# One core, attention and two MLP layers in one kernel: layer 1's first weights get a buffer of their own and load 17 steps earlier; their conversion, some scores and some value products change step

## The chip, the cores and the metric

The kernel runs on one NeuronCore of a Trainium2 chip. The metric is the time of one execution on the device in microseconds, lower is better. The engines are named as in the profile: PE is TensorE (matmul, with PEld for its weight loads), DVE is VectorE, ACT is ScalarE, POOL is GpSimd, SP is SyncE, which here only issues DMAs. Each engine takes its instructions in the order in which they stand in its own queue, and waits at an instruction until the semaphores that it needs are there.

## The reference, cut to what matters

```python
def _attn_ref(q, k, v, w_pre, w_post):                 # batch 2, heads 12, sequence 448, head_dim 64
    scores = scale * np.matmul(q, k.transpose(0, 1, 3, 2))
    scores = np.einsum('bhij,hg->bgij', scores, w_pre)  # mix the heads before the softmax
    scores = scores - np.max(scores, axis=-1, keepdims=True)
    attn = np.exp(scores)
    attn = attn / (np.sum(attn, axis=-1, keepdims=True) + 1e-09)
    attn = np.einsum('bhij,hg->bgij', attn, w_post)     # and after it
    return np.matmul(attn, v)

def _moe_ref(x, w_in, w_out):                           # layer 1: 896 tokens, 768 -> 2048 -> 768
    h = x @ w_in
    g = h * np.clip(h + 3.0, 0.0, 6.0) / 6.0
    return g @ w_out

def _moe2_ref(x, w_in, w_out, a, b):                    # layer 2, the same sizes, a rational activation
    h = x @ w_in
    ...
    return (P / (Q + 1e-6)) @ w_out
```

`reference` runs the three after one another. The weights of the layers come as float64 words; the kernel reads them as pairs of int32.

## The kernel before

**Attention** is done in 46 steps `m`. A step handles 20 query rows (two groups of ten) of all 12 heads. Steps belong to eight chunks of up to 120 rows; chunks 0 to 7 begin at steps 0, 6, 12, 18, 23, 29, 35 and 41. In step m PE does, in this order: `premix(m)` (eight matmuls into the two banks `M`), then a part of a later chunk's scores (`sc`, two head pairs, eight matmuls) or of an earlier chunk's value products (`X`, 32 matmuls), then `postmix(m-2)` (64 matmuls into the bank `A`). There are two banks `M`, so the premix of step m+1 writes what the exp of step m has read.

Around a premix the chain is: DVE takes the row maxima of both banks (`st`, two reduces), ACT takes two exps (`e`), DVE inverts the sums (`norm`: two short instructions on `st`), POOL scales the second mix (`wr`), PE does the postmix two steps later, ACT copies its result out (`at`, the evacuation). X leaves its bank through ACT (`xh`) and DVE (`xl`). Scores leave theirs through DVE copies into one of two buffers `stage0`, `stage1` (chunk number modulo 2), and DMAs issued on SP spread the rows of a stage into `first`, a ring of five step inputs; the spread for step m+4 is issued in step m. A stage is written for chunk C+2 when the spreads of chunk C have read it.

**Layer 1** is done by units. Unit u of the first kind (u0, u1, ... the 16 column blocks of `w_in`) is 768 KB of raw words (`wraw`), which ACT and DVE turn into float32 and then into a high and a low part:

```python
nc.scalar.activation(out=w, in_=hw.bitcast(F32), func=AF.Copy, scale=2.0**-112)      # ACT wf
nc.vector.tensor_scalar(out=wi, in0=wi, scalar1=3, ..., op0=ALU.logical_shift_left)  # DVE, first of three on wf
```

Two more DVE instructions on `wf` follow (called the second and third), and then `wh` and `wl`: on POOL for the first four units, on ACT and DVE for the others. `split_pieces` is a generator, and `PIECES` says how many of its pieces each step runs at its end; `LOADS` says in which step the thirds of a raw unit are loaded. `gemm1(f, p)` multiplies unit f with the tokens of part p (384 or 512 of them): six times three matmuls, called `h1_f_p`. Unit u0's raw words take one of two buffers `wraw` in a pool `late`, which is made in step 37, when a pool with queries and keys is given back.

The order of the steps and of the tail behind them (the last two postmixes, the value products X7 of the last chunk, first matmuls of layer 1) is written out by hand. From `manual.__exit__` on a scheduler places the instructions; it may also put later ones between earlier ones of an engine's queue.

Of the kernel before, what the change touches and what calls it, by code (L numbers as in the profile page):

```python
# [29 lines left out]
NP = H // 2  # L30
# [18 lines left out]
def fused_kernel(  # L49
# [287 lines left out]

    THIRDS = 3

    def load_third(u, i):  # L340
        u = units[u]
        if i == 0:
            raws[u] = (pools["late"].tile([128, KD * 256], I32, tag="wraw", bufs=2, name="wraw"), KD)
        n = KD // THIRDS
        o = raws[u][0].rearrange("p (a b) -> p a b", b=256)[:, i * n : i * n + n]
        nc.sync.dma_start(out=o, in_=w1i[:, i * n : i * n + n, u[1] * 256 : u[1] * 256 + 256])

    def load_unit(u, eng=nc.sync):
        kind, i, kk = u
        if kind == "in2" and i in pre:  # L350
            t = ring("wpre")[:, : KD * 128].bitcast(F32)
            eng.dma_start(out=t, in_=pre[i])
            raws[u] = (t, KD)
            return
        if "gp2" in pools:
            t = ring("wraw")
        else:
            t = pools["late"].tile([128, KD * 256], I32, tag="wraw", bufs=2, name="wraw")
        cols = slice(i * 256, i * 256 + 256)
        if kind in ("in1", "in2"):  # L360
# [135 lines left out]
    def per_step(items):  # L496
# [24 lines left out]
    for m in range(len(pairs)):  # L521
# [33 lines left out]
        for p in xs[1::2]:  # L555
            p()
        if m == FREE:
            front.release()
            pools["late"] = tc.alloc_tile_pool(name="late", bufs=1, side="right", reuse_waits="tile")
            wpieces = (p for u in units[:4] for p in split_pieces(u))  # L560
# [26 lines left out]
    pieces(1)  # L587
    att.release()
# [290 lines left out]
```

## Time and profile before

| | |
|---|---|
| median of 3 runs | 666.91 us (666.86 to 667.76) |
| the profiled execution | 665.91 us, span from first to last instruction 664.2 us |
| PE busy | 645.7 us, 97% of the span |
| DVE, ACT, POOL busy | 77%, 57%, 5% |
| steps 0 to 45 | from 15.27 to 185.24 us |
| tail | from 185.24 to 201.64 us |
| from then on | h1_0_1 and all that follows |

The profile's rows give a start in microseconds of the span, a length, an engine, a source line and the tiles (the number behind a tile's name left out); what stands in square brackets is the idle time of that engine just before, and what ended it.

### The profile page before, as it was taken

The numbers are of one execution on the slowest core, as the hardware profiler recorded it, in microseconds if no ns is written. First come the engines' busy times: TensorE is split into PE (matmuls) and PEld (weight loads), VectorE is DVE, ScalarE is ACT, GpSimd is POOL, SyncE is SP. The second block draws the span as 40 slices with busy tenths as digits, with TensorE's granted clock in tenths as the row PEclk, the third lists the DMA queues.
The fourth block names the chain that finished last, engine by engine and source line by source line (L and its number), as shares of the span: only waits on it lengthen the run. The fifth ranks groups of instructions, "written<-read, shape, count | busy, mean of one in ns | idle before, by whom it ended". The sixth has DMA issues, their size and how long they took to land.

```text
span 664.2 us, 16127 instructions
## 1 busy us (share of the span) xinstructions
PE 645.7 (97%) x6681; PEld 537.2 (81%) x6682; DVE 514.2 (77%) x880; ACT 377.6 (57%) x682; POOL 34.2 (5%) x73
## 2 busy tenths in 40 slices
PE   8899999997899999999999999999999999999997
PEld 3355665664587988998888888899999999999997
DVE  5777677774658988889686665389998999989991
ACT  3666676765645555555333232167675676689851
POOL 2110110111312000000000000000000000000000
PEclk9999999997999999999999999999999999999999
DMA  6765544536344655556645233446757564746512
GB/s 220 239 198 190 149 179 138 169 131 194 124 134 141 204 167 167 173 183 211 198 140 173 88 119 98 164 170 235 250 174 278 192 229 161 273 156 214 190 49 95
DMA packets 72281, 115.48 MB, mean 174 GB/s; under 512 B 6352, under 2 KB 56816, under 8 KB 72208
## 3 DMA queue, kind: packets, MB, share of 16 engines
q1 hardware_dynamic: 71790, 114.08, 52.1%
q8 instruction: 52, 0.85, 0.5%
q10 hardware_dynamic: 418, 0.37, 0.2%
q14 instruction: 21, 0.17, 0.1%
HBM read 75.39 MB, written 19.27 MB: 143 GB/s over the span
## 4 chain that ended last, share of the span: by engine, by line
PE 89%; DVE 4%; ACT 3%; DMA 2%; issue 1%; POOL 0%; SPq 0%; POOLq 0%; DVEq 0%; ACTq 0%
PE h L318 11%; PE h L319 11%; PE h L320 11%; PE y L318 6%; PE y L320 6%; PE acc L318 6%; PE acc L320 6%; PE acc L319 6%; PE y L319 6%; PE sc L216 6%; PE A L275 5%; PE X L298 5%; PE M L232 5%; ACT e L241 1%; DMA first<-stage 1%
## 5 line engine op out<-in xcount | busy, mean ns | idle before, releaser
L318 PE MATMUL h<-xh,wh 128*128 128x512 f32 (+1 forms) x384 | 140.2, 365 | 0.9 <-DVE g L488 0.9
L319 PE MATMUL h<-xl,wh 128*128 128x512 f32 (+1 forms) x384 | 140.1, 365 | 0.0
L320 PE MATMUL h<-xh,wl 128*128 128x512 f32 (+1 forms) x384 | 139.1, 362 | 0.0
L318 PEld LDWEIGHTS h<-xh,wh 128*128 128x128 f32 x384 | 72.1, 188 | 9.4 <-issue 1.3
L320 PEld LDWEIGHTS h<-xh,wl 128*128 128x128 f32 x384 | 72.1, 188 | 8.1
L319 PEld LDWEIGHTS h<-xl,wh 128*128 128x128 f32 x384 | 72.2, 188 | 6.6
L239 DVE TENSOR_REDUCE st<-M 128x1 f32<-128x448 f32 x92 | 53.3, 619 | 30.9 <-PE M L232 30.5
L241 ACT ACTIVATE e<-M,st 128x448 f32<-128x448 f32 x92 | 57.5, 629 | 34.3 <-DVE st L239 34.3
L376 ACT ACTIVATE wf<-wraw 128x768 f32<-128x768 f32 (+1 forms) x56 | 49.5, 883 | 45.3 <-DVE wl L404 36.9
L403 ACT ACTIVATE wh<-wf 128x768 fp32r<-128x768 f32 (+1 forms) x52 | 42.5, 817 | 50.5 <-PE y L319 38.1
L320 PE MATMUL y<-gh,wl 128*128 128x384 f32 x192 | 70.6, 368 | 0.0
L318 PE MATMUL y<-gh,wh 128*128 128x384 f32 x192 | 70.5, 367 | 0.0
L319 PE MATMUL y<-gl,wh 128*128 128x384 f32 x192 | 69.9, 364 | 0.0
L404 DVE TENSOR_TENSOR wl<-wf,wh 128x768 fp32r<-128x768 f32 (+1 forms) x52 | 48.0, 923 | 27.4 <-ACT wh L403 27.3
L275 PEld LDWEIGHTS A<-wr,e 60*56 60x56 f32 x2944 | 43.6, 127 | 21.7 <-issue 18.7
L232 PE MATMUL M<-first,wp 60*64 60x448 f32 (+1 forms) x368 | 50.0, 554 | 8.1 <-ACT e L241 7.8
L283 ACT COPY at<-A 120x960 f32<-120x960 f32 x46 | 45.0, 978 | 22.4 <-PE A L275 21.6
L380 DVE SCALAR_TENSOR_TENSOR wf<-wraw,icst,wf 128x768 int32<-128x768 int32 (+1 forms) x56 | 55.3, 989 | 0.8
L384 DVE SCALAR_TENSOR_TENSOR wf<-wraw,icst,wf 128x768 int32<-128x768 int32 (+1 forms) x56 | 55.3, 988 | 0.7
L220 DVE COPY stage<-sc 120x448 f32<-120x448 f32 (+1 forms) x85 | 49.1, 616 | 7.2 <-PE sc L216 4.5
L275 PE MATMUL A<-wr,e 60*56 60x60 f32 x2944 | 49.7, 216 | 2.5 <-ACT at L283 2.2
L298 PEld LDWEIGHTS X<-at,vraw 120*64 120x64 f32 x768 | 38.3, 140 | 16.4 <-DVE st L249 7.0
(99 smaller groups left out, 1137.5 us busy)
## 6 DMA issues: line engine op xcount, KB each, us to landing
wraw<-in_moe_w_out_dram SPq DMA_DIRECT2D x28, 768.0 KB
first<-stage SPq DMA_DIRECT2D x92, 210.0 KB
wraw<-in_moe_w_in_dram SPq DMA_DIRECT2D x18, 768.0 KB
wpre<-in_moe_w_in_dram SPq DMA_DIRECT2D x10, 768.0 KB
w2h<-wh SPq DMA_DIRECT2D x16, 384.0 KB
w2l<-wl SPq DMA_DIRECT2D x16, 384.0 KB
ws<-w2h SPq DMA_DIRECT2D x16, 384.0 KB
ws<-w2l SPq DMA_DIRECT2D x16, 384.0 KB
```

The costliest lines, as they stand in the source:

```text
L220: return [lambda copy, i=i: copy(out=st[:n, i], in_=sc[i][:n, :S]) for i in range(2)]
L232: nc.tensor.matmul(mt[a][64 * c : 64 * c + 64, :S], lhsT=wp[o], rhs=src[o, c, :], start=True, stop=True,)
L239: nc.vector.tensor_reduce(out=st[:, a : a + 1], in_=mt[a][:, :S], op=ALU.max, axis=AX.X, negate=True)
L241: nc.scalar.activation(out=e[:, a], in_=mt[a][:, :S], func=AF.Exp, bias=st[:, a : a + 1], accum_out=st[:, 2 + a : 3 + a])
L275: nc.tensor.matmul(av[64 * c : 64 * c + JH, r, jc, :, a * HR : a * HR + HR], lhsT=e[o, a, j : j + JH], rhs=wr[o, a], start=True, stop=True,)
L298: nc.tensor.matmul(X[hh % 2 * D : hh % 2 * D + D, hh % 4 // 2, :n], lhsT=vs[:, jc, :], rhs=at[C][:, jc, hh, :n], start=(jc == 0), stop=(jc ...
L318: nc.tensor.matmul(o, lhsT=wh, rhs=mh, start=first, stop=False)
L319: nc.tensor.matmul(o, lhsT=wh, rhs=ml, start=False, stop=False)
L320: nc.tensor.matmul(o, lhsT=wl, rhs=mh, start=False, stop=last)
L376: nc.scalar.activation(out=w, in_=hw.bitcast(F32), func=AF.Copy, scale=2.0**-112)
L380: nc.vector.scalar_tensor_tensor(out=wi, in0=hw, scalar=icst[:, 0:1], in1=wi, op0=ALU.bitwise_and, op1=ALU.bitwise_or)
L384: nc.vector.scalar_tensor_tensor(out=wi, in0=lw, scalar=icst[:, 1:2], in1=wi, op0=ALU.logical_shift_right, op1=ALU.bitwise_or)
```

## The change

- `raw0`, a buffer that is there from the start. Raw units alternate between it and one buffer in `late`. u0's thirds are loaded in steps 20, 21 and 22, u1's in 37 and 38, u2's in 39 and 40, u3's in 42 and 43. A step's load is now issued on SP ahead of the step's spread.
- The pieces are cut otherwise: (ACT wf), (first DVE), (second DVE), (third DVE with wh and wl). `PIECES` runs two a step from step 37 to 42 and one each in 44 and 45. Only three units have wh and wl on POOL; u3's go to ACT and DVE.
- `FILL`: h1_0_0 is done in halves of nine matmuls, at the ends of steps 41 and 42. The tail is first half of h1_1_0, postmix 44, second half, postmix 45, h1_2_0, X7, h1_0_1. Before it was h1_0_0, postmix 44, half of h1_1_0, postmix 45, the other half, X7, h1_2_0, h1_0_1.
- `SCORES`: chunk 2's six pairs, one a step in steps 2 to 7 (before two a step in 3, 5 and 7); chunk 4's in 15, 17 and 18 (before 14, 16 and 18). Chunk 2's queries are loaded ahead of the first spreads.
- `VALUES`: X of chunk 1 in steps 14 and 16 (before 15 and 17); X of chunk 5 in 38, 39 and 40 (before 38, 40 and 42).

```diff
-    pools = {}
+    pools = {"raw0": tc.alloc_tile_pool(name="raw0", bufs=1, side="right")}
...
+    turn = [0]
+
+    def raw_tile():
+        turn[0] += 1
+        return pools[("late", "raw0")[turn[0] % 2]].tile([128, KD * 256], I32, tag="wraw", bufs=1, name="wraw")
...
-            raws[u] = (pools["late"].tile([128, KD * 256], I32, tag="wraw", bufs=2, name="wraw"), KD)
+            raws[u] = (raw_tile(), KD)
...
             out=wi, in0=lw, scalar=icst[:, 1:2], in1=wi, op0=ALU.logical_shift_right, op1=ALU.bitwise_or
         )
-        yield
...
-        if u in units[:4]:
+        if u in units[:3]:
...
         spl[u] = (hv, lv)
+        yield
...
-    for m in range(3):
-        spread_pair(m)
     load_q(2)
-    for m in range(3, RING):
+    for m in range(RING):
         spread_pair(m)
...
-    SCORES = [begin[C] - i for C in range(2, NC) for i in (9, 7, 5)]
-    VALUES = [8, 10, 12, 15, 17, 19, 21, 23, 25, 27, 29, 31, 33, 35, 37, 38, 40, 42, 43, 44, 45]
+    SCORES = [9, 11, 13, 15, 17, 18, 20, 22, 24, 26, 28, 30, 32, 34, 36]
+    VALUES = [8, 10, 12, 14, 16, 19, 21, 23, 25, 27, 29, 31, 33, 35, 37, 38, 39, 40, 43, 44, 45]
...
-    PIECES = dict(zip(range(38, 46), (1, 2, 2, 2, 1, 2, 2, 1)))
-    LOADS = {37: ((0, 0), (0, 1), (0, 2)), 38: ((1, 0), (1, 1)), 39: ((1, 2),)}
-    LOADS.update({40: ((2, 0),), 41: ((2, 1), (2, 2)), 43: ((3, 0), (3, 1)), 44: ((3, 2),)})
+    PIECES = {37: 2, 38: 2, 39: 2, 40: 2, 41: 2, 42: 2, 44: 1, 45: 1}
+    LOADS = {20 + i: ((0, i),) for i in range(THIRDS)}
+    LOADS.update({37: ((1, 0), (1, 1)), 38: ((1, 2),), 39: ((2, 0),), 40: ((2, 1), (2, 2))})
+    LOADS.update({42: ((3, 0),), 43: ((3, 1), (3, 2))})
+    FILL = {41: (0, 3), 42: (0, 3)}
...
+        if m in FILL:
+            f, n = FILL[m]
+            if f not in early:
+                early[f] = gemm1(f, 0, ps.tile([128, 512], F32, tag="sc", bufs=BUFS["sc"], name=f"h1_{f}_0"))
+            for _ in range(n):
+                next(early[f])
...
-    run(gemm1(0, 0, ps.tile([128, 512], F32, tag="sc", bufs=BUFS["sc"], name="h1_0_0")))
-    postmix(m - 2)
-    at_evac(m - 2, acopy)
     h110 = gemm1(1, 0, ps.tile([128, 512], F32, tag="sc", bufs=BUFS["sc"], name="h1_1_0"))
     for _ in range(3):
         next(h110)
+    postmix(m - 2)
+    at_evac(m - 2, acopy)
+    run(h110)
     postmix(m - 1)
     at_evac(m - 1, acopy)
-    pieces(1)
-    run(h110)
+    run(gemm1(2, 0, ps.tile([128, 512], F32, tag="sc", bufs=BUFS["sc"], name="h1_2_0")))
     for i in range(NP):
         tail_x(2 * i + 1, "sc" if i < 2 else "M")
-    run(gemm1(2, 0, ps.tile([128, 512], F32, tag="sc", bufs=BUFS["sc"], name="h1_2_0")))
```

On DVE, in steps 2 and 3, before the change (`st2` and `st3` are the steps' maxima and norms, `sc2_0` and `sc2_1` the first pair of chunk 2):

```order
L239 TENSOR_REDUCE st2_313<-M2_0_307 128x1
L239 TENSOR_REDUCE st2_313<-M2_1_308 128x1
L248 TENSOR_SCALAR st2_313<-st2_313 128x2
L249 RECIPROCAL st2_313<-st2_313 128x2
L239 TENSOR_REDUCE st3_367<-M3_0_361 128x1
L239 TENSOR_REDUCE st3_367<-M3_1_362 128x1
L220 COPY stage0_127<-sc2_0_375 120x448
L220 COPY stage0_127<-sc2_1_376 120x448
```

The same place after it:

```order
L239 TENSOR_REDUCE st2_316<-M2_0_310 128x1
L239 TENSOR_REDUCE st2_316<-M2_1_311 128x1
L220 COPY stage0_127<-sc2_0_324 120x448
L220 COPY stage0_127<-sc2_1_325 120x448
L248 TENSOR_SCALAR st2_316<-st2_316 128x2
L249 RECIPROCAL st2_316<-st2_316 128x2
L239 TENSOR_REDUCE st3_376<-M3_0_370 128x1
L239 TENSOR_REDUCE st3_376<-M3_1_371 128x1
```

The first copies into `stage0` for chunk 2 now stand a step earlier, ahead of step 2's norm and step 3's reduces.

On ACT, in steps 37 to 39, before the change (`at6` is the evacuation, `wf` the first instruction of unit u0's conversion):

```order
L283 COPY at6_2648<-A_177 120x2x48x10
L241 ACTIVATE e38_2707,st38_2706<-M38_0_2700,st38_2706 128x448
L241 ACTIVATE e38_2707,st38_2706<-M38_1_2701,st38_2706 128x448
L310 ACTIVATE xh_129<-X5_1_2712 128x2x120
L283 COPY at6_2648<-A_177 120x2x48x10
L376 ACTIVATE wf_2770<-wraw_2696 128x768
L241 ACTIVATE e39_2782,st39_2781<-M39_0_2775,st39_2781 128x448
L241 ACTIVATE e39_2782,st39_2781<-M39_1_2776,st39_2781 128x448
```

And after it:

```order
L283 COPY at6_2655<-A_177 120x2x48x10
L381 ACTIVATE wf_2706<-wraw_1533 128x768
L241 ACTIVATE e38_2716,st38_2715<-M38_0_2709,st38_2715 128x448
L241 ACTIVATE e38_2716,st38_2715<-M38_1_2710,st38_2715 128x448
L310 ACTIVATE xh_129<-X5_1_2721 128x2x120
L283 COPY at6_2655<-A_177 120x2x48x10
L241 ACTIVATE e39_2793,st39_2792<-M39_0_2786,st39_2792 128x448
L241 ACTIVATE e39_2793,st39_2792<-M39_1_2787,st39_2792 128x448
```

u0's `wf` has moved from the end of step 38 to the end of step 37, and reads a tile that was loaded in steps 20 to 22.

On ACT, around step 45's exps after the change (`wf_3208` is u3's, `wf_3559` is u4's; before the change both stood behind step 45's evacuation):

```order
L283 COPY at7_3098<-A_177 120x2x48x10
L381 ACTIVATE wf_3208<-wraw_3047 128x768
L241 ACTIVATE e45_3217,st45_3216<-M45_0_3210,st45_3216 128x448
L381 ACTIVATE wf_3559<-wraw_3508 128x768
L241 ACTIVATE e45_3217,st45_3216<-M45_1_3211,st45_3216 128x448
L310 ACTIVATE xh_129<-X6_9_3222 128x2x120
```

The scheduler has put u4's conversion between the two exps of the last step; its three DVE instructions stand around that step's norm.

## Rows read from the trace of the kernel before

**Rows 1.** The page: busy time by engine.

```profile
PE 645.7 (97%) x6681; PEld 537.2 (81%) x6682; DVE 514.2 (77%) x880; ACT 377.6 (57%) x682; POOL 34.2 (5%) x73
```

**Rows 2.** Busy time in stretches (start:end, length, engines), clock, DMA share, GB/s.

```profile
157.67:164.32 6.65, 6.65 (x105) 4.63 (x108) 3.64 (x10) 3.14 (x8) 0.92 (x2) 0.56 0.67 205
201.64:215.11 13.47, 12.53 (x56) 9.99 (x55) 11.08 (x16) 6.57 (x10) 3.51 (x2) 1.00 0.52 151
244.16:258.63 14.47, 14.47 (x73) 13.00 (x72) 13.19 (x19) 8.06 (x13) 0.00 (x0) 1.00 0.51 160
```

**Rows 3.** Timeline, steps 37 to 42.

```profile
147.69 0.94 PE L232 MATMUL M<-first,wp 64*64 64x448 f32 x8
147.94 0.98 ACT L283 COPY at<-A 120x960 f32<-120x960 f32 x1 [0.41 <-PE A L275]
148.76 1.16 DVE L239 TENSOR_REDUCE st<-M 128x1 f32<-128x448 f32 x2 [0.75 <-PE M L232]
149.48 0.63 ACT L241 ACTIVATE e<-M,st 128x448 f32<-128x448 f32 x1 [0.56 <-DVE st L239]
...
152.61 1.06 PE L275 MATMUL A<-wr,e 60*56 60x60 f32 x64 [0.41 <-ACT at L283]
156.11 0.89 ACT L376 ACTIVATE wf<-wraw 128x768 f32<-128x768 f32 x1 [3.65 <-DMA wraw<-in_moe_w_in_dram]
157.67 2.38 PE L232 MATMUL M<-first,wp 64*64 64x448 f32 x8 [4.00 <-ACT e L241]
158.55 0.54 DVE L378 TENSOR_SCALAR wf<-wf 128x768 int32<-128x768 int32 x1
159.13 1.02 DVE L380 SCALAR_TENSOR_TENSOR wf<-wraw,icst,wf 128x768 int32<-128x768 int32 x1
166.89 0.62 ACT L241 ACTIVATE e<-M,st 128x448 f32<-128x448 f32 x1
167.04 1.59 PE L232 MATMUL M<-first,wp 64*64 64x448 f32 x8 [0.28 <-ACT e L241]
```

**Rows 4.** Timeline, steps 43 to 45 and the tail.

```profile
177.29 1.83 POOL L401 TENSOR_TENSOR wl<-wf,wh 128x768 fp32r<-128x768 f32 x1
177.71 1.82 DVE L378 TENSOR_SCALAR wf<-wf 128x768 int32<-128x768 int32 x1 [1.54 <-ACT wf L376]
...
180.94 1.59 PE L232 MATMUL M<-first,wp 64*64 64x448 f32 x8 [1.61 <-ACT e L241]
182.45 1.86 PE L298 MATMUL X<-at,vraw 120*64 120x120 f32 x32
185.24 0.44 PE L318 MATMUL h<-xh,wh 128*128 128x384 f32 x1
...
188.56 1.06 PE L275 MATMUL A<-wr,e 60*56 60x60 f32 x64
194.62 3.86 PE L298 MATMUL X<-at,vraw 120*64 120x88 f32 x96
```

**Rows 5.** Timeline, first matmuls of layer 1 after the tail.

```profile
201.64 0.39 PE L318 MATMUL h<-xh,wh 128*128 128x512 f32 x1
215.11 0.42 PE L318 MATMUL h<-xh,wh 128*128 128x384 f32 x1 [0.94 <-DVE g L488]
```

**Rows 6.** The chain that ended last (start, length, what), steps 2 and 3.

```profile
20.93 6.23 DMA first<-stage
27.43 1.16 DVE stage L220 x2
```

**Rows 7.** Timeline, step 4 and the start of step 9.

```profile
27.25 0.94 PE L232 MATMUL M<-first,wp 64*64 64x448 f32 x8
28.78 1.14 DVE L239 TENSOR_REDUCE st<-M 128x1 f32<-128x448 f32 x2
44.97 0.56 PE L232 MATMUL M<-first,wp 64*64 64x448 f32 x4
```

**Rows 8.** Timeline, step 14.

```profile
65.17 1.54 PE L216 MATMUL sc<-keys,qraw 64*120 64x448 f32 x4 [0.92 <-DVE stage L220]
```

More of the change, by code (lines that the diff above doesn't have):

```diff
@@ L357, in load_unit @@
         else:
-            t = pools["late"].tile([128, KD * 256], I32, tag="wraw", bufs=2, name="wraw")
+            t = raw_tile()
         cols = slice(i * 256, i * 256 + 256)
@@ L502, in fused_kernel @@
     NC = len(chunks)
-    SCORES = [begin[C] - i for C in range(2, NC) for i in (9, 7, 5)]
-    VALUES = [8, 10, 12, 15, 17, 19, 21, 23, 25, 27, 29, 31, 33, 35, 37, 38, 40, 42, 43, 44, 45]
-    SC = per_step([(0, (1, hp)) for hp in range(FIRST, NP)] + list(zip(
-        sorted(2 * SCORES), [(C, hp) for C in range(2, NC) for hp in range(NP)])))
+    SCORES = [9, 11, 13, 15, 17, 18, 20, 22, 24, 26, 28, 30, 32, 34, 36]
+    VALUES = [8, 10, 12, 14, 16, 19, 21, 23, 25, 27, 29, 31, 33, 35, 37, 38, 39, 40, 43, 44, 45]
+    SC = per_step([(0, (1, hp)) for hp in range(FIRST, NP)] + [(2 + hp, (2, hp)) for hp in range(NP)] + list(zip(
+        sorted(2 * SCORES), [(C, hp) for C in range(3, NC) for hp in range(NP)])))
     XS = per_step(list(zip(
@@ L512, in fused_kernel @@
     FREE = max(SC) + 1
-    PIECES = dict(zip(range(38, 46), (1, 2, 2, 2, 1, 2, 2, 1)))
-    LOADS = {37: ((0, 0), (0, 1), (0, 2)), 38: ((1, 0), (1, 1)), 39: ((1, 2),)}
-    LOADS.update({40: ((2, 0),), 41: ((2, 1), (2, 2)), 43: ((3, 0), (3, 1)), 44: ((3, 2),)})
+    PIECES = {37: 2, 38: 2, 39: 2, 40: 2, 41: 2, 42: 2, 44: 1, 45: 1}
[3 more added lines that the diff above has]
+    FILL = {41: (0, 3), 42: (0, 3)}
+    early = {}
     def pieces(n):
@@ L545, in fused_kernel @@
             p(vcopy)
+        if m == FREE:
+            front.release()
+            pools["late"] = tc.alloc_tile_pool(name="late", bufs=1, side="right", reuse_waits="tile")
+            wpieces = (p for u in units[:4] for p in split_pieces(u))
+        for x in LOADS.get(m, ()):
+            load_third(*x)
         if 1 <= m <= len(pairs) - RING:
@@ L556, in fused_kernel @@
             p()
[L557 to L560, printed above, removed]
         pieces(PIECES.get(m, 0))
-        for x in LOADS.get(m, ()):
-            load_third(*x)
+        if m in FILL:
[4 more added lines that the diff above has]
+                next(early[f])
     m = len(pairs)
@@ L577, in fused_kernel @@
         next(h110)
+    postmix(m - 2)
+    at_evac(m - 2, acopy)
+    run(h110)
     postmix(m - 1)
     at_evac(m - 1, acopy)
-    pieces(1)
-    run(h110)
+    run(gemm1(2, 0, ps.tile([128, 512], F32, tag="sc", bufs=BUFS["sc"], name="h1_2_0")))
     for i in range(NP):
         tail_x(2 * i + 1, "sc" if i < 2 else "M")
-    run(gemm1(2, 0, ps.tile([128, 512], F32, tag="sc", bufs=BUFS["sc"], name="h1_2_0")))
     h101 = ps.tile([128, 512], F32, tag="M", bufs=BUFS["M"], name="h1_0_1")
     run(gemm1(0, 1, h101))
-    pieces(1)
     att.release()
@@ L594, in fused_kernel @@
     act1(2, 0)
-    pieces(2)
     run(gemm1(1, 1, ps.tile([128, 512], F32, tag="M", bufs=BUFS["M"], name="h1_1_1")))
@@ L825, in fused_kernel @@
     pools["late"].release()
+    pools["raw0"].release()
     xp.release()
```

## The prediction

> **What bounds the kernel now.** I read the page first, then the busy time in stretches, then the timeline where PE waits. On the page PE is busy for 97% of the span [rows 1], so some 18 us of idle PE and whatever the clock loses are all that an edit of the order can win. The stretches show where. From 201.64 to 215.11 PE is busy for 12.53 of 13.47 us, and later, from 244.16 to 258.63, all the time [rows 2]. So there a change helps only by starting this part earlier, and hurts as soon as a weight is late: DVE is busy for 13.19 of those 14.47 us, 91%. The timeline of steps 37 to 42 shows the largest wait: premix 40 starts at 157.67 after 4.00 us of idle PE. It waited for an exp, and the exp for the instruction ahead of it on ACT, u0's `wf`, which waited 3.65 us for a load that was issued only in step 37 [rows 3]. The stretch behind it ran at a granted clock of 0.56 of full speed, near the lower level of 1.2 GHz: the premix at 157.67 took 2.38 us against 1.59 for one gated in the same way at 167.04 [rows 2, 3]. A second wait, 1.61 us ahead of premix 45, comes from DVE's first `wf` instruction, which took 1.82 us at 177.71 while POOL's `wl` ran from 177.29 to 179.12 [rows 4].
>
> **Steps 37 to 45.** I walk the steps by the distances in [rows 3]. From a premix's start the reduces follow after 1.07 us (147.69 to 148.76), the first exp 0.72 later; the second exp 0.62 after the first. The next premix can start when the first exp has ended and end some 1.7 after the second exp's start (166.89 to 168.63, where ends are modelled and overlap the next start a little). I count 0.78 from exp to premix, 1.67 for its end, 1.79 for an X (182.45 to the postmix behind it, ahead of 185.24) and 0.9 to 1.06 for a postmix [rows 4].
>
> Nothing changes up to premix 38 at 147.7. The evacuation ends at 148.92, and now u0's `wf` (0.89 to 0.91) stands behind it with its words long there: 149.84. DVE's first `wf` instruction (0.54) ends at 150.45, and step 38's reduces, which had started at 148.76, start then. Exp 151.17, premix 39 at 151.95 (before 151.24), X and postmix done at 156.14. In step 38 DVE does the norm, `xl`, and then the second and third instruction, twice 1.02, to 155.30; the reduces of step 39 start there, the exp at 156.02, premix 40 at 156.80. So the 4.00 us wait is gone, but each step of the conversion makes its successor's reduces 1.2 to 1.7 us late and leaves PE idle for about 0.7. Going on in the same way premixes 41 to 45 start at 161.6, 166.4, 171.0, 175.4 and 179.6, and postmix 43 ends at 183.19. By then h1_0_0 is done, in the PE time of steps 41 and 42, which have no X. Before, it ended at 188.56 (185.24 plus 3.32) [rows 4]. **Gain so far: 188.56 - 183.19 = 5.37.** It is made of 4.00 and 1.61 of waits and about 2.4 of lost clock (the stretch from 157.67 took 6.65 for a premix, an X and a postmix, 1.59 + 1.79 + 0.89 at the full clock, [rows 2]), 8.0 in all, less the new idle moments.
>
> POOL's `wl` (1.83) now runs while norms 39, 41 and 43 come up on DVE. If each waits for its end as the instruction at 177.71 did, that is about 0.7 each; in the walk it lies beside ACT's `wf`, on which the next reduces wait anyway. Without that cover it would cost up to 2.1.
>
> **Tail.** From 183.19 PE does half of h1_1_0 (1.55), waits 0.8 for evacuation 43 behind u4's `wf` on ACT, then postmix 44, the other half, postmix 45 (188.85), h1_2_0 (3.1, as h1_0_0) and X7 (3.8, [rows 4]), to 195.75. h1_0_1 starts there instead of at 201.64 [rows 5]: **5.89** in all, 0.52 more than above.
>
> **What is late next.** Three products with the 512-token part (before, the 12.53 of PE's time in [rows 2], 12.4 without the overlap of ends) bring PE to 208.2, where h1_3_0 needs u3's `wl`. That was POOL's work; now it stands on DVE behind h1_1_1's activation. h1_1_1 ends at 204.0; from there ACT's and DVE's instructions for it, the third `wf` instruction, `wh` and `wl` follow: on DVE three at the mean of 0.69 (11.08 us for 16, [rows 2]) and the third and `wl` at 1.02 each, on ACT two at 0.66 (6.57 for 10). That is 5.4 us end to end, up to 0.9 more with the handovers between the engines: 209.4 to 210.3. PE waits 1.2 to 2.1, before 0.94 [rows 5]: **0.3 to 1.2 given back, I take 0.7.** u5's words wait for the buffer that u3 frees, one of two; its `wl` comes up to 0.6 later than h1_5_0 wants it: **0.35**. Together this part is worth -5.89 + 0.7 + 0.35 = **-4.84**, with bounds of -5.6 and -4.1.
>
> **Steps 2 to 9.** The first copy of chunk 2 overwrites `stage0`, which the last spread of chunk 0 still reads. That spread was issued up to 20.93 and landed at 27.16; the copy started at 27.43 [rows 6]. It stood behind step 3's reduces; now it stands ahead of step 2's norm and step 3's reduces, which wait with it. Chunk 2's queries, loaded ahead of the first spreads, leave the queue a little earlier: I take 26.5 for the copy's start, between 25.7 (most of that load's time won) and 27.43 (none). Two copies and the norm took 27.43 to 28.78 [rows 6, 7], 1.35 to 1.45; the reduces then start at 27.95, the exp at 28.67, premix 4 at 29.45 instead of 27.25 [rows 7]. PE has nothing from about 26.6 on: 2.8 us idle (2.0 to 3.8). Behind that each step has one pair where every second had two, so PE's work lies better beside DVE's: the walk takes 16.0 us from premix 4 to premix 9, the trace 17.72. Premix 9 comes at 45.44 against 44.97: **+0.5**, bounds -0.3 and +1.4 by those of the copy's start.
>
> **The rest.** Step 14's copies of two chunks met, and PE lost 0.92 [rows 8]; the same four meet in step 18 now: **0**, between -0.5 and +0.5, one such loss less or half of another. The early thirds of u0 stand ahead of a spread that has four steps to land: 0, and up to 1 if the queue backs up.
>
> **Sum.** -4.84 + 0.5 + 0 = -4.3. The walk is on the profiled execution, 665.91, which is 1.0 below the median; the same difference on the median of 666.91 gives **662.6**.
>
> **The rivals.**
> *The clock falls in the new idle of steps 3 and 4.* Before, PE stopped at 153.67 (152.61 plus 1.06) and the premix at 157.67 ran slow; after 1.61 us ahead of premix 45 it did not [rows 3, 4]. 2.8 us lies half-way between. The price was 2.4: 662.6 + 2.4 = 665.0. For it: steps 2 to 9 leave PE idle more often than step 39 did. Against it: PE's short waits have stayed without one. Chance 0.23. The Trainium skill, "TensorE: Matmul & The Clock Gate", section "HAM oscillation — how this bites in real kernels", says that a PE that waits too long between bursts is throttled and starts the next one cold. The trace agrees at 157.67. By that rule alone the new idle might cost the same again, and the sum would be this rival's.
> *The wait only moves.* The load's wait is gone, but DVE's conversion (2.6 us a unit in two steps) and POOL's lock come on the path: the 2.1 above without cover, and 0.5 of idle more in some steps: 662.6 + 2.6 = 665.2. For it: the 1.82 at 177.71. Against: before, the same instructions stood in steps 39 to 44 and premixes 42 to 44 came without such a wait. Chance 0.17.
> *Slower: layer 1 becomes bound by DVE.* The scheduler converts u5 and u6 side by side, and all units are wanted 5 us sooner by a DVE that is 91% busy. If each of some ten units' `wl` is late by over 0.45 us, the 4.3 are gone; at 0.6 it is 662.6 + 6 = 668.6. Against: DVE has 1.28 us of slack in two units, so a lag of one unit is caught up. Chance 0.09.
> *u4's words have not landed* when ACT comes to its `wf` between the exps of step 45: by the walk issued near 174 and needed near 182; before, u0's words, loaded in step 37 behind 147.7, were there at 156.11 [rows 3], with others beside them. ACT, and the exp behind it, would wait 1 to 2: 664.1. Chance 0.06.
>
> **How the numbers follow.** The forecast as it stands has 0.45, with 661.3 to 663.6 by the bounds. The first, second and fourth rivals reach to 665.2, with their own spread to 666.5; below 660 lies only a sum with every bound on the good side. The range of 659.8 to 666.4 leaves out the third rival and a tenth of the others. 0.2%, 1.3 us, is about what a measurement of this kernel can tell from none: faster means under 665.6, slower over 668.2. The forecast and the fourth rival are faster: 0.51. The first two, 0.40 together, lie at 1.7 under the time before, close to the bound of 1.3: 0.24 of them faster, 0.15 the same, 0.01 slower. The third gives slower: 0.09. Faster 0.75, same 0.15, slower 0.10.
>
> **What would show it.** ACT's first `wf` on unit words without a wait near 149; no fall of the granted clock at 158; premix 40 near 157, the first matmul of h1_0_0 near 164 and h1_0_1 near 196; an idle PE of 1 to 2 ahead of h1_3_0; a copy that waits for `first` near 26 in step 2, premix 4 near 29.4, the clock at 1.00 behind it. It is wrong if premix 9 is later than 46.5, if the granted clock falls in the first 40 us, if h1_0_1 is later than 198, or if PE waits again and again behind 220.

## The result, and the profile after

| | before | changed |
|---|---|---|
| median (4 runs each, same chip) | 667.34 us (666.86 to 670.43) | 659.10 us (657.42 to 659.53) |
| ratio | | 0.9862, 95% interval 0.9827 to 0.9897 |
| profiled execution | 665.91 us, span 664.2 us | 659.53 us, span 657.1 us |

The changed kernel is faster by 1.4%. The forecast of faster held; the time lies 0.7 us below the range's lower end of 659.8. The spans differ by 7.1 us, the medians by 8.2. Further runs of the kernel before went from 664.6 to 673, so the last microsecond of the medians can be scatter, and the account below goes by the 7.1 us between the profiled executions. One execution of e5 below, the profiled one, took 716.53 us at a mean granted clock of 0.847; it is left out of e5's row, and its profile is not used.

The changed kernel's page, busy time by engine and the granted clock in 40 slices, answers to [rows 1]:

```profile
PE 646.7 (98%) x6681; PEld 536.1 (82%) x6682; DVE 513.7 (78%) x881; ACT 378.9 (58%) x683; POOL 31.1 (5%) x71
...
PEclk9899999999999999999999999999999999999999
```

PE does the same work in a shorter span: what it isn't busy in has gone from 18.5 us (664.2 less 645.7) to 10.4. The 8 in the second slice is new, and is taken up below.

Busy time of the changed kernel in stretches (start:end, length, then PE, PEld, DVE, ACT and POOL, granted clock, DMA share, GB/s), as in [rows 2]:

```profile
20.00:24.00 4.00, 3.83 (x36) 1.41 (x40) 1.57 (x4) 2.07 (x8) 0.39 (x1) 0.73 0.78 238
24.00:28.00 4.00, 4.00 (x130) 2.62 (x124) 2.94 (x8) 1.90 (x4) 0.39 (x1) 0.84 0.75 226
156.57:161.08 4.51, 4.37 (x105) 2.95 (x105) 2.94 (x6) 3.29 (x8) 1.79 (x2) 1.00 0.67 209
194.97:207.46 12.49, 12.49 (x56) 10.11 (x55) 10.18 (x17) 7.34 (x14) 0.00 (x0) 1.00 0.18 49
```

Step 40 (156.57 to 161.08) took 4.51 us at the full clock, where it took 6.65 at 0.56 before, close to the lower of the two levels, 1.2 GHz of 2.4. The three products from h1_0_1 to h1_3_0 now have no idle PE at all.

Timeline of steps 38 to 40 of the changed kernel, against [rows 3]:

```profile
147.73 0.94 PE L232 MATMUL M<-first,wp 64*64 64x448 f32 x8
147.97 0.97 ACT L283 COPY at<-A 120x960 f32<-120x960 f32 x1 [0.40 <-PE A L275]
148.85 0.93 ACT L381 ACTIVATE wf<-wraw 128x768 f32<-128x768 f32 x1
149.81 0.56 DVE L383 TENSOR_SCALAR wf<-wf 128x768 int32<-128x768 int32 x1 [1.76 <-ACT wf L381]
150.28 1.15 DVE L239 TENSOR_REDUCE st<-M 128x1 f32<-128x448 f32 x2
...
151.77 1.58 PE L232 MATMUL M<-first,wp 64*64 64x448 f32 x8 [0.32 <-ACT e L241]
...
152.96 1.15 DVE L385 SCALAR_TENSOR_TENSOR wf<-wraw,icst,wf 128x768 int32<-128x768 int32 x1
154.14 1.02 DVE L389 SCALAR_TENSOR_TENSOR wf<-wraw,icst,wf 128x768 int32<-128x768 int32 x1
155.08 1.15 DVE L239 TENSOR_REDUCE st<-M 128x1 f32<-128x448 f32 x2
...
156.16 1.81 POOL L405 TENSOR_TENSOR wl<-wf,wh 128x768 fp32r<-128x768 f32 x1
...
156.57 1.59 PE L232 MATMUL M<-first,wp 64*64 64x448 f32 x8 [0.42 <-ACT e L241]
157.16 0.84 DVE L248 TENSOR_SCALAR st<-st 128x2 f32<-128x2 f32 x1 [0.94 <-ACT e L241]
```

u0's `wf` starts with no wait, right behind the evacuation, and the two reduces that follow wait for the conversion on DVE. PE pays 0.32 and 0.42 us for it, in place of 4.00 us and a slow stretch.

Timeline of the tail and of layer 1's start, against [rows 4, 5]; the first row is the fill in step 41, the next u4's `wf` between step 45's exps. A row with x2 stands for two instructions of the same kind, one behind the other; at 207.39 they are the `wl` of u3 and that of u4:

```profile
163.91 0.45 PE L318 MATMUL h<-xh,wh 128*128 128x384 f32 x1
...
181.22 0.91 ACT L381 ACTIVATE wf<-wraw 128x768 f32<-128x768 f32 x1
...
182.33 0.44 PE L318 MATMUL h<-xh,wh 128*128 128x384 f32 x1
...
194.97 0.51 PE L318 MATMUL h<-xh,wh 128*128 128x512 f32 x1
...
207.39 1.83 DVE L408 TENSOR_TENSOR wl<-wf,wh 128x768 fp32r<-128x768 f32 x2 [0.31 <-ACT wh L407]
207.46 0.39 PE L318 MATMUL h<-xh,wh 128*128 128x384 f32 x1
...
208.41 0.44 PE L320 MATMUL h<-xh,wl 128*128 128x384 f32 x1 [0.37 <-DVE wl L408]
...
211.28 0.39 PE L318 MATMUL h<-xh,wh 128*128 128x512 f32 x1
...
222.65 0.34 PE L318 MATMUL h<-xh,wh 128*128 128x384 f32 x1
```

h1_0_1 starts 6.67 us sooner than in [rows 5], h1_3_0 7.65 sooner and with a wait of only 0.37. h1_3_1, at 211.28 against 218.31, is 7.03 sooner, and behind it the kernel runs as before: 445.8 to 445.9 us to the end in both.

So the change can be told apart by the starts of a few premixes (M2 is that of step 2) and of h1_3_1. Each cell is the difference of two starts in one profile:

| kernel | M2 to M14 | M14 to M19 | M19 to M38 | M38 to h1_3_1 | h1_3_1 to h1_5_1 |
|---|---|---|---|---|---|
| before | 41.68 | 19.16 | 66.18 | 70.62 | 14.48 |
| changed | 41.10 | 19.62 | 66.84 | 63.56 | 14.48 |
| e1, weights only | 43.26 | 19.15 | 65.68 | 63.54 | 15.03 |
| e2, early load only | 42.11 | 19.15 | 65.85 | 66.54 | 14.48 |
| e3, without the fill | 42.83 | 19.62 | 66.30 | 67.44 | 14.74 |
| e4, u3 on POOL | 42.79 | 19.56 | 66.96 | 65.44 | 14.48 |
| e6, changed again | 42.10 | 19.56 | 67.09 | 63.56 | 14.48 |
| e7, scores from step 3 | 44.15 | 19.55 | 65.58 | 63.54 | 14.48 |
| e8, filler in step 1 | 43.19 | 19.56 | 66.61 | 63.56 | 14.65 |
| e9, u0 loaded in step 37 | 42.22 | 19.61 | 66.36 | 63.51 | 14.48 |
| e10, two moves | 43.62 | 18.55 | 65.68 | 63.58 | 14.48 |
| e11, two moves and filler | 40.69 | 18.55 | 66.01 | 63.56 | 14.65 |

The column from M38 to h1_3_1 is steady to 0.07 us wherever the weight part is that of the changed kernel. The attention columns scatter by up to 1.7 us with the same code there (M2 to M14 in changed, e3, e4, e6 and e9).

### The profile page after: what moved, and what is told of

It is laid out like the page before. It is cut to its first block, busy times and chain, and to the rows that moved or that the text cites. A ratio compares the mean times of both kernels' runs of the same rounds, so it can differ in the third digit from the quotient of the medians.

```text
span 657.1 us, 16134 instructions
## 1 busy us (share of the span) xinstructions
PE 646.7 (98%) x6681; PEld 536.1 (82%) x6682; DVE 513.7 (78%) x881; ACT 378.9 (58%) x683; POOL 31.1 (5%) x71
## 4 chain that ended last, share of the span: by engine, by line
PE 94%; DVE 2%; ACT 2%; issue 1%; DMA 1%; SPq 0%; ACTq 0%; DVEq 0%
PE h L318 12%; PE h L319 11%; PE h L320 11%; PE A L275 7%; PE y L318 6%; PE y L320 6%; PE acc L318 6%; PE acc L319 6%; PE acc L320 6%; PE y L319 6%; PE sc L216 6%; PE M L232 6%; PE X L298 5%; ACT e L241 1%; DVE st L239 1%
## 5 line engine op out<-in xcount | busy, mean ns | idle before, releaser
L232 PE MATMUL M<-first,wp 64*64 64x448 f32 (+1 forms) x368 | 51.0, 547 | 2.5 <-ACT e L241 2.1
L298 PEld LDWEIGHTS X<-at,vraw 120*64 120x64 f32 x768 | 36.9, 137 | 15.5 <-DVE st L249 5.6
```

The source lines that it names most:

```text
L232: nc.tensor.matmul(mt[a][64 * c : 64 * c + 64, :S], lhsT=wp[o], rhs=src[o, c, :], start=True, stop=True,)
L298: nc.tensor.matmul(X[hh % 2 * D : hh % 2 * D + D, hh % 4 // 2, :n], lhsT=vs[:, jc, :], rhs=at[C][:, jc, hh, :n], start=(jc == 0), stop=(jc ...
```

## The experiments

Times in us; the ratio is to runs of the kernel before on the same chip, with its 95% interval.

| run | median (lowest to highest) | ratio |
|---|---|---|
| e1, weights only | 659.78 (658.62 to 660.81) | 0.9897 (0.9859 to 0.9935) |
| e2, early load only | 663.39 (660.63 to 667.73) | 0.9951 (0.9922 to 0.9980) |
| e3, without the fill | 665.65 (662.10 to 671.12) | 0.9995 (0.9964 to 1.0026) |
| e4, u3 on POOL | 662.72 (659.44 to 665.23) | 0.9927 (0.9902 to 0.9953) |
| e5, attention moves only | 667.52 (664.78 to 670.34) | 1.0006 (0.9982 to 1.0030) |
| e6, changed again | 660.16 (658.74 to 663.12) | 0.9892 (0.9862 to 0.9923) |
| e7, scores from step 3 | 658.23 (657.19 to 661.83) | 0.9865 (0.9832 to 0.9899) |
| e8, filler in step 1 | 661.14 (660.86 to 661.49) | 0.9904 (0.9872 to 0.9935) |
| e9, u0 loaded in step 37 | 659.41 (658.59 to 661.82) | 0.9880 (0.9837 to 0.9924) |
| e10, two moves | 657.61 (656.60 to 660.39) | 0.9845 (0.9808 to 0.9882) |
| e11, two moves and filler | 658.34 (656.75 to 659.89) | 0.9856 (0.9821 to 0.9891) |

**e1: the weight part alone.** The changed kernel with the order of the early scores and of chunk 1's X as before, and chunk 2's queries loaded where they were. The X of chunk 5 stays moved.

```diff
+    for m in range(3):
+        spread_pair(m)
     load_q(2)
-    for m in range(RING):
+    for m in range(3, RING):
         spread_pair(m)
...
-    SCORES = [9, 11, 13, 15, 17, 18, 20, ...]
-    VALUES = [8, 10, 12, 14, 16, 19, ...]
...
+    SCORES = [3, 5, 7, 9, 11, 13, 14, 16, 18, 20, ...]
+    VALUES = [8, 10, 12, 15, 17, 19, ...]
...
```

> The changed kernel with the scores of chunks 2 and 4, the value products of chunk 1 and the load of chunk 2's queries put back to their old places; all that concerns layer 1's weights, the fill and the tail stays changed. By the prediction's sum (weights -4.8, early scores +0.5) it takes 0.5 less than the changed kernel on the same footing: 4.8 under before, premix 38 where before had it (147.7), h1_3_0 near 210. By the theory read from the two traces (weights -7.0, the other edits cancel) it takes 7 under before, 659 to 660, h1_3_1 near 211.3, and what it shows at premix 38 against the changed kernel is run-to-run scatter of the first 15 us and of single issue gaps, under 1 us.

**e5: the attention moves alone**, on the kernel before.

```diff
-    for m in range(3):
-        spread_pair(m)
     load_q(2)
-    for m in range(3, RING):
+    for m in range(RING):
         spread_pair(m)
...
-    SCORES = [begin[C] - i for C in range(2, NC) for i in (9, 7, 5)]
-    VALUES = [8, 10, 12, 15, 17, 19, ...]
...
+    SCORES = [9, 11, 13, 15, 17, 18, 20, ...]
+    VALUES = [8, 10, 12, 14, 16, 19, ...]
+    SC = per_step([...] + [(2 + hp, (2, hp)) for hp in range(NP)] + ...
...
```

> The kernel before with the attention edits alone: chunk 2's scores one pair a step in steps 2 to 7, their queries loaded first, chunk 4's scores in 15, 17, 18 and chunk 1's value products in 14 and 16. The prediction has +0.5 for this part (premix 9 later by 0.5, the meeting of copies moved from step 14 to 18 for 0). By the traces so far the distance from premix 2 to premix 14 is 41.1 to 42.8 with the new places and 41.7 to 43.3 with the old ones, so 0 within a scatter of 1, and the distance from premix 14 to 19 is 0.45 longer with the new ones: same as before within 0.2%, +0.5 in the profile from premix 2 to 38 but for single issue gaps.

e1 has the whole gain of the column from M38 (63.54) and, within the intervals, that of the time; e5 has none in its time. So the gain is the weight part's.

**e2: the early load alone.** The kernel before with `raw0` and u0's thirds in steps 20 to 22; pieces, fill and u3's engine as before.

```diff
...
-    LOADS = {37: ((0, 0), (0, 1), (0, 2)), 38: ((1, 0), (1, 1)), 39: ((1, 2),)}
+    LOADS = {20: ((0, 0),), 21: ((0, 1),), 22: ((0, 2),), 38: ((1, 0), (1, 1)), 39: ((1, 2),)}
```

> The kernel before with one edit: u0's thirds go to a buffer of their own and are loaded in steps 20 to 22; pieces, tail, scores and value products stay as before. If the gain is the load's wait and the clock loss behind it, ACT's first wf no longer waits, premix 40 starts near 154.2 instead of 157.7, the clock stays at 1.00 and the end of h1_0_0 comes 3.5 to 4.5 sooner; the tail then keeps its old waits: 662.5 to 663.5. If the gain is the new packing (pieces by twos, fill, order of the tail), this kernel gains under 2. If the wait only moves to DVE and POOL, premixes 42 to 45 show new idle PE of over 1 us each and the gain is under 2.5.

From M38 it gains 4.08 us. Premixes 38, 40, 42 and 45 in its timeline, and the X behind premix 42:

```profile
146.91 0.94 PE L232 MATMUL M<-first,wp 64*64 64x448 f32 x8
...
153.15 1.59 PE L232 MATMUL M<-first,wp 64*64 64x448 f32 x8 [0.27 <-ACT e L241]
...
161.68 1.58 PE L232 MATMUL M<-first,wp 64*64 64x448 f32 x8 [1.74 <-ACT e L241]
163.19 3.30 PE L298 MATMUL X<-at,vraw 120*64 120x120 f32 x32
...
176.07 1.59 PE L232 MATMUL M<-first,wp 64*64 64x448 f32 x8 [0.92 <-ACT e L241]
```

Step 40 comes 6.24 us behind step 38, where it came 9.98 behind in [rows 3]; then 1.74 and 0.92 us are paid at premixes 42 and 45, and the X behind the first of these waits takes 3.30 us where others take 1.86. By itself, with the new waits that it brings, the early load is worth 4 of the 7 us; what else is gained needs the rest of the change.

**e3: without the fill.** The changed kernel with h1_0_0 back behind the last step.

```diff
-    FILL = {41: (0, 3), 42: (0, 3)}
+    FILL = {}
...
+    run(gemm1(0, 0, ps.tile([128, 512], F32, tag="sc", bufs=BUFS["sc"], name="h1_0_0")))
     h110 = gemm1(1, 0, ...)
```

> The changed kernel without the fill: h1_0_0 stands ahead of h1_1_0 in the tail again instead of in halves in steps 41 and 42. If the fill puts 3.1 us of PE's work into time that was idle anyway, premixes 42 to 45 start where they do in the changed kernel (165.9, 170.2, 174.5, 178.7) and h1_0_1 comes 3.1 later (198.1): 3.1 over the changed kernel. If the idle time in steps 41 and 42 was mostly taken by the fill from the steps behind (they start later because of it), it costs under 1.5. Behind h1_0_1 the later products wait less for u3's weights, by the 0.4 that the changed kernel still shows.

3.88 us of the 7.06 are lost: 3.23 are h1_0_0 itself, back in the tail (184.83 to 188.06), the rest is lost in the steps. Premixes 42 to 44 in its timeline:

```profile
167.60 1.58 PE L232 MATMUL M<-first,wp 64*64 64x448 f32 x8 [1.86 <-ACT e L241]
171.84 1.59 PE L232 MATMUL M<-first,wp 64*64 64x448 f32 x8 [1.60 <-ACT e L241]
177.65 0.93 PE L232 MATMUL M<-first,wp 64*64 64x448 f32 x8
```

And its busy time in stretches around them (columns as above):

```profile
168.00:172.00 4.00, 2.40 (x74) 1.31 (x72) 2.62 (x5) 2.78 (x7) 1.39 (x2) 1.00 0.75 236
172.00:176.00 4.00, 4.00 (x36) 2.87 (x36) 3.38 (x6) 1.82 (x5) 2.07 (x3) 0.68 0.03 7
```

The two halves of h1_0_0, 3.1 us of work, had stood in idle time of 1.86 and 1.60 us. With that time idle again the granted clock falls to 0.68, a mean over parts at either level, and step 43 takes 5.81 us (171.84 to 177.65) where it took 4.32 with the fill; 0.66 of that comes back in step 44, which takes 3.53 in place of 4.19. So the fill also holds the clock up: in e2, which has no fill either, it fell in the same steps, and in the changed kernel it is 1.00 from 164 to 180 us. The Trainium skill ("TensorE: Matmul & The Clock Gate", "HAM oscillation — how this bites in real kernels") says that a PE that waits too long between bursts is throttled and starts the next one cold; the trace agrees here, where the slow step stands behind the two waits.

**e4: u3 on POOL again.** The changed kernel with one number as before.

```diff
-        if u in units[:3]:
+        if u in units[:4]:
```

> The changed kernel with u3's wh and wl on POOL again, as before the change. By the prediction the move to ACT and DVE gave back 0.3 to 1.2 at h1_3_0, so with POOL the wait there is that of before (0.9) or less and the time about 0.7 less than the changed kernel. By the theory from the traces POOL's wl (1.8 to 2.4) and wh (0.8 to 1.1) end later than ACT and DVE do (208.3), since u3's third instruction ends at 206.5: 206.5 + 0.1 + 1.0 + 2.1 = 209.7, so h1_3_0 waits 1.4 to 2 longer and the kernel is 1 to 2 us slower than the changed one.

It loses 1.88 us. POOL's two instructions for u3 and the two waits of h1_3_0 in its timeline:

```profile
208.64 1.13 POOL L404 TENSOR_SCALAR wh<-wf 128x768 fp32r<-128x768 f32 x1 [21.20 <-DVE wf L389]
209.83 0.44 PE L318 MATMUL h<-xh,wh 128*128 128x384 f32 x1 [0.20 <-POOL wh L404]
209.86 2.39 POOL L405 TENSOR_TENSOR wl<-wf,wh 128x768 fp32r<-128x768 f32 x1
212.30 0.44 PE L320 MATMUL h<-xh,wl 128*128 128x384 f32 x1 [1.85 <-POOL wl L405]
```

`wh` and `wl` take 1.13 and 2.39 us on POOL one behind the other. In the changed kernel they also stand one behind the other, but are shorter: u3's `wh` takes 0.85 us on ACT, from 206.51, and its `wl` 0.96 on DVE, from 207.39. The prediction had counted this move as a loss.

In time e3 and e4 lose more than the column from M38 shows: their medians lie 5.9 and 2.9 us above e1's on the same chip, where the column has 3.90 and 1.90, and e3's time cannot be told from that of the kernel before. Why they lose more stays open.

**e9: u0 loaded in step 37 after all**, into its own buffer; the issue stands ahead of step 37's spread.

```diff
-    LOADS = {20 + i: ((0, i),) for i in range(THIRDS)}
-    LOADS.update({37: ((1, 0), (1, 1)), 38: ((1, 2),), 39: ((2, 0),), 40: ((2, 1), (2, 2))})
+    LOADS = {37: ((0, 0), (0, 1), (0, 2))}
+    LOADS.update({38: ((1, 0), (1, 1), (1, 2)), 39: ((2, 0),), 40: ((2, 1), (2, 2))})
```

> The changed kernel with u0's three thirds loaded in step 37 and u1's in step 38, still into the buffer that is there from the start and ahead of the step's spread. If the early place (steps 20 to 22) is what takes the wait away, ACT's first wf waits as long as before (3.6 us or more, the clock falls again) and the kernel loses most of 4 us of the changed kernel's gain. If it is enough that the load stands ahead of step 37's spread, which waits until 147.5 for the last copies of chunk 7, the thirds are issued from 143.4 on (u1's first two are, in the changed kernel) and land near 150: ACT's first wf waits 1 to 2 us, premix 39 comes that much later, and the kernel is 1 to 2 slower than the changed one.

It gains the same, 63.51 from M38; neither of the two outcomes expected came. SP's DMA issues and u0's `wf` in its timeline:

```profile
141.64 1.51 SPq L351 DMA_DIRECT2D wraw<-in_moe_w_in_dram  x3
148.69 1.70 SPq L207 DMA_DIRECT2D first<-stage  x2
150.00 0.92 ACT L381 ACTIVATE wf<-wraw 128x768 f32<-128x768 f32 x1
```

SP runs ahead of the other engines: the load is issued at 141.64, while step 37's spread waits until 148.69 for the copies that it reads. Behind that spread the load is issued only then, as the timeline of the kernel before shows:

```profile
149.24 3.90 SPq L346 DMA_DIRECT2D wraw<-in_moe_w_in_dram  x3
```

So it is the place ahead of the spread, with a buffer that is free, that takes the wait away; the 17 steps between 20 and 37 bring nothing more. The place counts for more of it than the buffer: u1's first two thirds, which in the changed kernel go ahead of the same spread into the buffer in `late`, were issued at 143.44. What the place alone gives, without the new buffer, was not run.

**e6: the changed kernel again**, unaltered, to see what one profile of it is worth.

> The changed kernel unaltered, on the same chip as the others of this call and timed in more rounds. If the first timing (8 us under before) was partly the scatter of a few runs, it takes 6.5 to 7.5 under before, as the two profiles had it by their spans (7.1); if the profiles understate it, 8 to 9.

The weight column is 63.56 again; the attention columns differ by up to 1.0. The median is 7.3 us under that of the kernel before on this chip, and at 660.16 it lies inside the range forecast.

**e7: chunk 2's scores from step 3.**

```diff
-    SCORES = [9, 11, 13, 15, 17, 18, 20, ...]
+    SCORES = [9, 11, 13, 15, 18, 20, ...]
...
-    ... [(2 + hp, (2, hp)) for hp in range(NP)] ...
-        sorted(2 * SCORES), ...
+    ... [(s, (2, hp)) for hp, s in enumerate((3, 4, 5, 6, 6, 7))] ...
+        sorted(2 * SCORES + [16, 17]), ...
```

> The changed kernel with two more moves: chunk 2's pairs in steps 3, 4, 5, 6, 6, 7, so that no copy stands ahead of step 3's reduces while the last spread of chunk 0 is still landing, and chunk 4's pairs in 15, 15, 16, 17, 18, 18, so that no four copies meet in step 18 behind a pair of steps with two. If the copy of step 2 is what holds premix 4 (27.9 to 28.6 in the changed kernel's order), premix 4 follows premix 2 by 6.0 to 6.6 instead of 7.7 to 7.8 and premix 14 by 40 to 40.5: 1 to 2 less. If PE's 0.92 ahead of the scores of step 18 comes from the four copies, it is gone and the distance from premix 14 to 19 falls from 19.6 to 18.7. Together 2 to 3 under the changed kernel; if both waits only move, within 0.5 of it.

It was meant to take away the copy's wait in step 2 and the jam of copies in step 18. Premix 4 came 8.20 behind M2 (7.69 in the changed kernel), M2 to M14 was not shorter in its profile (44.15), and the jam had only moved, to 0.92 us in step 16 (M14 to M19 19.55). The time cannot be told from the changed kernel's.

**e8: a filler in step 1**, behind the premix, to test whether the idle PE ahead of M2 is what lets the clock fall. Its four matmuls are extra work; nothing uses their result.

```diff
+        if m == 1:
+            pw = ps.tile([128, 512], F32, tag="sc", ...)
+            for i in range(4):
+                nc.tensor.matmul(pw, lhsT=warm[:, :128], rhs=warm, start=(i == 0), stop=(i == 3))
```

> The changed kernel with four bf16 matmuls of 512 columns on memory that is zero, into a bank of their own, behind premix 1, where PE else waits 1.34 us for an exp; their result is used by nothing. If that idle time is why the granted clock fell in steps 2 to 5 in four of six profiles and the fall costs 1 to 1.7 from premix 2 to premix 14, the clock stays at 1.00 there and that distance is 41.1 or less. If the fall comes from the whole thin stretch, it falls in this kernel too. If the waits for DVE hide it, the distance stays near 41 whatever the clock does.

Inconclusive: with it the clock stayed at 1.00 from 20 to 28 us and fell to 0.71 from 28 to 32, behind two new waits of 0.72 and 0.97 us. M2 to M14 is 43.19, the time as without it.

**e10 and e11: both moves**, e7 and the second X step of chunk 1 in step 17 instead of 16; e11 has e8's filler too.

```diff
-    VALUES = [8, 10, 12, 14, 16, 19, ...]
+    VALUES = [8, 10, 12, 14, 17, 19, ...]
```

> The kernel with chunk 2's pairs in 3, 4, 5, 6, 6, 7 and chunk 4's in 15, 15, 16, 17, 18, 18, and the second value products of chunk 1 in step 17 instead of 16, so that held scores, a new pair and X's bank do not meet in step 16 (there PE waited 0.92 in the run before this). The distance from premix 14 to 19 falls from 19.55 to 18.6 to 18.9; the time is 1 to 3 under the changed kernel (657 to 658.5), of which some 1.5 comes from steps 2 to 9.

> The kernel of e10_both_moves with four bf16 matmuls of 512 columns on zeros behind premix 1, whose result nothing uses. In e8 the same matmuls kept the clock up to 28 us and it fell there, behind two new waits of 0.7 and 1.0; chunk 2's pairs from step 3 on should leave no such waits. If the fall of the clock in steps 2 to 8 costs 1 to 2, the distance from premix 2 to premix 14 is 40.0 to 40.6 with a clock of 1.00 throughout and the time 1 to 2 under e10; if the thin stretch loses its clock anyway, or the loss is hidden, the same time as e10 within 0.5.

The jam is gone in both: M14 to M19 18.55, 1.1 less than in the changed kernel. Busy time and clock of e10 in steps 2 and 3 (columns as above):

```profile
20.00:24.00 4.00, 3.05 (x52) 1.80 (x56) 2.23 (x6) 2.07 (x6) 0.54 (x2) 0.66 0.75 241
```

The same stretch of e11:

```profile
20.00:24.00 4.00, 3.81 (x80) 2.02 (x80) 2.26 (x7) 2.86 (x8) 0.73 (x2) 1.00 0.82 215
```

e11's profile has the full clock there where e10's has 0.66, and the shortest M2 to M14 of all, 40.69; over six runs it is no faster than e10. e10 is the fastest version found, 657.61 us, but its interval overlaps that of the changed kernel, so it is not shown to be faster.

## Why the prediction was right in the cause and short in the size

The mechanism was the one predicted. The term that failed is the weight part, put at -4.84 with bounds of -5.6 and -4.1; it measured **-7.06**. The other terms of the sum, 0.5 and 0, came to about 0 (M38 at 147.73 against 147.69); that they did so to 0.04 is luck, for in e6, the same program, M38 is at 149.99.

**Steps 37 to 45: -5.89 up to h1_0_1, measured -6.67.** The walk found each wait where it is, but gave each step too much:

| start of | walk | trace |
|---|---|---|
| premix 39 | 151.95 | 151.77 |
| premix 40 | 156.80 | 156.57 |
| premix 42 | 166.4 | 165.85 |
| premix 45 | 179.6 | 178.68 |
| h1_1_0 | 183.19 | 182.33 |
| h1_0_1 | 195.75 | 194.97 |

It is late by some 0.1 us more a step. Rows overlap where one instruction hands over to the next on its engine: the third `wf` instruction starts at 154.14 and takes 1.02, and the reduce behind it starts at 155.08, not 155.16; the evacuation at 147.97 takes 0.97, and `wf` starts at 148.85. I had laid lengths end to end. That is 0.78 us of the 2.2.

**What is late next: +0.7 and +0.35, measured -0.36 and 0.** This was the larger error, and had the wrong sign. I had u3's `wl` ready at 209.4 to 210.3 and PE waiting for it from 208.2; its reader started at 208.41, with 0.37 us of wait. Three things were off. PE came to h1_3_0 at 207.46, 0.7 sooner, which is the walk's error again. The first two matmuls of h1_3_0 need only `wh`, so PE came to `wl` at 208.04. And I had counted all that DVE and ACT do for h1_1_1 and u3 as one chain of 5.4 us from 204.0 on, plus handovers; in the trace ACT's work stood beside DVE's. DVE's and ACT's instructions in the changed kernel's timeline (`gl` is the last of h1_1_1's, the first `wh` is u3's):

```profile
205.47 1.01 DVE L389 SCALAR_TENSOR_TENSOR wf<-wraw,icst,wf 128x768 int32<-128x768 int32 x1
206.40 0.68 DVE L494 TENSOR_TENSOR gl<-g,gh 128x512 fp32r<-128x512 f32 x1
206.51 1.58 ACT L407 ACTIVATE wh<-wf 128x768 fp32r<-128x768 f32 x2 [0.90 <-DVE wf L389]
```

The 0.94 before was another wait: [rows 5] has it on DVE's `g`, and POOL's `wl` for u3 had ended at 209.39. e4 shows the sign: on POOL the same work costs 1.88 us more. u5's lateness of 0.35 did not come: its `wl` ended at 222.38 (221.43 plus 0.95), and h1_5_0 ran from 222.65 without a wait. The term exists, though: PE waited 0.28 there in e1, where the same DVE instructions ran some 1.0 us later behind h1_3_1, after an ACT that had waited 2.53 us for a load (1.26 in the changed kernel), and the last column of the table is longer by 0.55. Together these make 1.41 of the error.

The runs split the 7.06 otherwise than the walk did. Alone, the early load is worth 4.08; taken out of the changed kernel, the fill costs 3.88 and u3's move 1.88. These are 9.84 together, more than the whole, so they don't add up: the fill stands in waits (1.86 and 1.60 us in e3) that the kernel before does not have in these steps, where no premix waits longer than 0.28 us. What the new cut of the pieces, the order of the tail and the moved X of chunk 5 are worth by themselves was not measured.

**POOL's lock** was right, and hidden as predicted. The norm at 157.16 took 0.84 us, till 158.00, with POOL's `wl` till 157.97; so did those of steps 41 and 43. No premix waited for it.

**Steps 2 to 9: +0.5, measured about 0.** Timeline of the changed kernel's steps 2 to 4, against [rows 6, 7]:

```profile
20.17 1.58 PE L232 MATMUL M<-first,wp 64*64 64x448 f32 x8 [1.34 <-ACT e L241]
21.69 1.75 PE L216 MATMUL sc<-keys,qraw 64*120 64x448 f32 x4
23.37 1.86 PE L275 MATMUL A<-wr,e 60*56 60x60 f32 x64
...
27.86 1.58 PE L232 MATMUL M<-first,wp 64*64 64x448 f32 x8
```

DVE's first copy of chunk 2 in the same steps:

```profile
25.03 1.16 DVE L220 COPY stage<-sc 120x448 f32<-120x448 f32 x2 [2.58 <-DMA qraw<-in_q_dram]
```

The copy did wait in step 2, but started at 25.03, before the earliest that I had allowed (25.7), and premix 4 came at 27.86 instead of 29.45. The row puts the wait down to a load of queries, but by the trace's semaphore events the last spread of chunk 0, issued at 19.90, landed at 24.75, 0.28 ahead of the copy; before, it landed at 27.16, 0.27 ahead [rows 6]. So the wait is the one predicted. It was shorter because the spread went out 1.03 us sooner and took 4.85 us instead of 6.23. From premix 4 to premix 9, at 43.86, it took the 16.0 us of the walk; premix 9 is 1.1 us sooner than before, outside the bounds given, and 0.5 of it is M2's earlier start. That is scatter too: premix 9 stands 22.8 to 25.4 us behind M2 in the five profiles of this order, 24.3 before. Over M2 to M14 the kernels with the old order have 41.68, 43.26 and 42.11, and those with the changed kernel's (changed, e3, e4, e6 and e9; e8 has the filler besides) 41.10 to 42.83: nothing to tell apart.

**Chunk 4's jam: 0, measured +0.45.** M14 to M19 is 19.15 to 19.16 in three profiles with the old order and 19.56 to 19.62 in six with the new one. The loss of 0.92 [rows 8] is there again, in step 18, and there is a new wait ahead of the X that now stands in step 14:

```profile
62.55 1.86 PE L298 MATMUL X<-at,vraw 120*64 120x120 f32 x32 [0.34 <-ACT at L283]
...
78.53 1.54 PE L216 MATMUL sc<-keys,qraw 64*120 64x448 f32 x4 [0.92 <-DVE stage L220]
```

The whole is within the bounds of 0.5 given.

**The rivals.** *The clock falls in steps 3 and 4*: it did fall, to 0.73 and 0.84 in the two stretches shown, so the text's own sign of being wrong was there; but its price of 2.4 was not paid. The slow scores and postmix above (1.75 and 1.86 against 1.02 and 1.06 at full clock) ran while DVE's copy was waiting anyway: the scores were done by 23.44, and the spread that the copy waited for landed at 24.75. In e6 the clock stayed at 1.00 and M2 came 1.08 later (21.25); there that spread landed at 24.89, the same copy started at 25.16, and premix 4 at 27.99, 0.13 behind the changed kernel's. DVE's copy in e6's timeline:

```profile
25.16 1.16 DVE L220 COPY stage<-sc 120x448 f32<-120x448 f32 x2 [1.63 <-DMA qraw<-in_q_dram]
```

*The wait only moves*: no; premixes 39 to 41 lose at most 0.42 us each. *Layer 1 becomes bound by DVE*: no; from h1_3_1 to h1_5_1 it takes 14.48 us in both kernels. *u4's words late*: no; `wf` at 181.22 did not wait.

M19 to M38 is 0.66 longer in the changed kernel, but from 65.58 to 67.09 over all, where these steps' order hardly differs. Part of it are gaps inside postmixes that the profile puts down to "issue", as in the changed kernel's timeline:

```profile
99.52 0.43 PE L275 MATMUL A<-wr,e 60*56 60x60 f32 x16 [0.99 <-issue]
```

Such gaps fall on other steps in other profiles, of the same code too. Their cause stays open.

## What to carry to other kernels

A load that an engine waits for may be late because of what stands ahead of it in the issuing queue: give it a buffer that is free, and put its issue ahead of the DMA that blocks, before moving it by many steps. Work that needs nothing new belongs into the idle time that a conversion leaves on PE; it saves its own length and keeps the clock from falling. When a walk over a timeline is made, take distances between starts of rows, not lengths laid end to end, and don't add two engines' work into one chain without the waits that force it.

## What the runs showed of the hardware that was not expected

- After an idle PE of 1.34 us ahead of M2 the granted clock fell to 0.73 from 20 to 24 us in the changed kernel; after the same 1.34 us it stayed at 1.00 in e6, the same program. One idle moment of this length, then, does not decide it. What does, in steps 2 to 4, stays open; e8 and e11 did not settle it.
- POOL's `wl` took 1.81 to 1.83 us in the steps and 2.39 at 209.86 in e4, beside a DVE busy with layer 1.
